# Nine unread 128x128 products placed between the products of a kernel's first chunk

## The chip, the cores and the metric

The kernel runs on one core of a Trainium2 chip. The metric is the device time of one execution in microseconds. The kernel before has a median of 508.19 us over three runs (507.17 to 508.34).

## The reference, cut to what matters

Two blocks run one after the other. The first is a delta-rule recurrence over 768 steps for 4 batches and 8 heads of 48 dimensions; the second is a feed-forward layer whose hidden value is the largest of three products.

```
k_n = k / (norm(k) + 1e-6)
for t in range(768):
    y[t]  = q[t] @ state
    v_old = state.T @ k_n[t]
    state = state + beta[t] * outer(k_n[t], v[t] - v_old)
x   = y laid out as 3072 tokens by 384
h   = max(max(x @ w1, x @ w2), x @ w3)      # 384 -> 768
out = h @ w_out                              # 768 -> 384
```

All of it is in 32-bit floating point; the weights come as 64-bit numbers, whose halves the kernel joins to 32 bits by itself.

## The kernel before, in words

The sequence is cut into 12 chunks of 64 steps. Within a chunk the recurrence becomes a triangular system: the inverse of a 64x64 triangle per head, then a few small products. Two chunks make a group of 512 tokens, and there are six groups; while the feed-forward layer of one group runs (`ffn(m)`), the recurrence of the next is threaded between its products.

The order of all instructions is written out by hand (`tc.manual_schedule()`): each engine takes its instructions in the order in which the Python code issues them. The part that matters here is the stretch before the first feed-forward group, and that group's first steps:

- `gram(n, ...)` (L404) makes the products of keys and queries (`p_g`). The last of them ahead of the stretch are those of L1343 and L1344.
- `solve(0)` (L507) eliminates in blocks of 16 on VectorE (`tmp`, L561; `y_bl`, L565), turns the result (L573), and places it in `ut` (L505).
- `halves_z(0)` and `halves_u(0)` (L676, L690) join blocks of 16 to blocks of 32 with two rounds of 64 small matmul records (`p_e`, `p_f`); `join_z(0)` and `join_u(0)` (L706, L719) join those to the inverse of 64 (`p_z`, `p_j`). Between the rounds ScalarE and VectorE copy the results out of PSUM (L688, L700, L717, L728).
- `new(0)` (L765) makes `u` (`p_u`), `to_y(0)` (L805) makes `y` (`p_y`), and `to_x(0)` (L819) turns `y` by six transposes (`p_x`) and copies it into `xt` (L839).
- `solve(1)` prepares the elimination for the second group on VectorE (L270 to L547). Its steps (L561, L565 on `y_p`) then run through the whole of the first feed-forward group.
- `ffn(0)` (L1213) starts with `hidden(0, ...)`: `p_h` (L1224) of 128x256, three matmuls (six records) for each of the three weights. The table `FIRST` (L1408) puts other work between: after the first `p_h` come `e1` (`p_e` of chunk 1) and `s0` (`p_s`, L794, with the VectorE sum into the state at L801) and two steps of `solve(1)`; after the second come `f1` (`p_f`), `k1` (`p_k`, L743, with VectorE's subtraction at L755) and three more steps.
- `weights()` (L230) joins the halves of the weights: three ScalarE operations (L247 to L249) for a piece, then one on VectorE (L259) and one on GpSimd (L263).

A 32-bit matmul stands in the profile as two records, each with its own weight load; a transpose stands as one. `ps_ffn` hands out two PSUM buffers in turn; `p_h` uses them later.

The kernel already has a helper, `busy(n, of)` (L1290), called once, with `busy(6, ident)` at L1309: six matmuls of the identity with itself into a tile `p_w` that nothing reads.

Of the kernel before, what the change touches and what calls it, by code (L numbers as in the profile page):

```python
# [23 lines left out]
def kernel(  # L24
# [31 lines left out]
    nc = tc.nc  # L56
# [10 lines left out]
    TOK = 512  # L67
# [21 lines left out]
    def ps_ffn(shape, name):  # L89
        return psum.tile(shape, FP32, name=name, tag="ffn", bufs=2)  # L90
# [10 lines left out]
    ident = const.tile([128, 128], FP32, name="ident")  # L101
# [16 lines left out]
    def rows(bb):  # L118
        return slice(C * bb, C * (bb + 1))
# [196 lines left out]
    def square(name):  # L316
        return work.tile([128, H, C], FP32, name=name, tag="square", bufs=17)
# [134 lines left out]
    def in_rows(t):  # L452
        return t.rearrange("p s r -> p (s r)")[:, 0 : BL * BL].rearrange(
            "p (j i) -> p j i", i=BL
        )
# [42 lines left out]
    def placed(cc, i, copy=nc.vector.tensor_copy, xs_of=slice(0, 2 * H)):  # L498
        bb, half = divmod(i, 2)
        r = block(bb, half)  # L500
        to = ut[cc][r, :, :, BL * half : BL * (half + 1)].rearrange(
            "p g h i -> p (g h) i"
        )
        of = in_rows(xs[0])[r, :, 16 * cc : 16 * (cc + 1)].rearrange("p i x -> p x i")
        copy(to[:, xs_of], of[:, xs_of])  # L505
# [110 lines left out]
    def both(name, w, bufs=1):  # L616
        return work.tile([128, 2, H, w], FP32, name=name, bufs=bufs)
# [6 lines left out]
    def block(bb, f=0, n=BL):  # L624
        return slice(C * bb + BL * f, C * bb + BL * f + n)

    def turn_t1(c):

        t, u_t = t1[c % NU], ut[c % NU]
        nc.vector.transpose(out=t[:, 0], in_=u_t[:, 0, :, 0:BL])  # L630
        for bb in range(2):
            nc.vector.transpose(
                out=t[block(1 - bb), 1], in_=u_t[block(bb), 1, :, 0:BL]
            )
# [4 lines left out]
    def halves_t(c, parts=(0, 1)):  # L639
        if c not in fine:  # L640
            fine[c] = [square("t") for g in range(2)]
        src = [ut[c % NU][:, g].rearrange("p h x -> p (h x)") for g in range(2)]
        dst = [t.rearrange("p h x -> p (h x)") for t in fine[c]]
        if 0 in parts:
            nc.vector.transpose(out=dst[0], in_=src[0])
        for bb in range(2) if 1 in parts else ():
            nc.vector.transpose(out=dst[1][rows(1 - bb)], in_=src[1][rows(bb)])

    def heads_of(c, name, w):


        copies = (nc.scalar.copy,) if c else (nc.scalar.copy, nc.vector.tensor_copy)
        n = H // len(copies)
        for i, copy in enumerate(copies):
            p_v = ps_two(name)[:, :, 0 : n * w]
            yield (
                range(i * n, i * n + n),
                p_v.rearrange("p g (h x) -> p g h x", x=w), copy,
            )
# [13 lines left out]
    def span(hs):  # L673
        return slice(hs[0], hs[-1] + 1)

    def halves_z(c):  # L676
        if c > 1:
            halves_t(c)
        at = [ats[2 * c + g] for g in range(2)]
        second = ut[c % NU].rearrange("p g h (f two x) -> p g h f two x", two=2, x=HB)  # L680
        for hs, p_v, copy in heads_of(c, "p_e", BL):
            for i, h in enumerate(hs):
                for bb, g in TILES:
                    r = rows(bb)
                    nc.tensor.matmul(
                        p_v[rows(bb ^ g), g, i], at[g][r, h], second[r, g, h, :, 1]
                    )
            copy(zs[c % NU][:, :, span(hs)], p_v)  # L688
# [17 lines left out]
    def join_z(c):  # L706
        at = [ats.pop(2 * c + g) for g in range(2)]
        z, second = zs[c % NU], ut[c % NU][:, :, :, BL:C]
        for hs, p_v, _ in heads_of(c, "p_z", BL):
            for i, h in enumerate(hs):  # L710
                for bb, g in TILES:
                    r = block(bb, 1)
                    nc.tensor.matmul(
                        p_v[block(bb ^ g), g, i], at[g][r, h, 0:BL], second[r, g, h]
                    )
            for bb in range(2):
                nc.scalar.copy(z[block(bb), :, span(hs)], p_v[block(bb)])  # L717
# [15 lines left out]
    def heads(t):  # L733
        return t.rearrange("p g (j two) d -> p two (g j) d", two=2)

    def times_state(kqt, i, name):
        p_b = ps_two(name)
        for j in range(NP):
            for g in range(2):
                for par in range(2):  # L740
                    for bb in range(2):
                        c0 = (g * NP + j) * D
                        nc.tensor.matmul(  # L743
                            p_b[rows(bb), par, c0 : c0 + D],
                            kqt[g][dims(par), j, bb ^ g, i],
                            st[dims(par), bb ^ g, g, j],
                        )
        return p_b[:, :, 0 : H * D].rearrange("p two (x d) -> p two x d", d=D)
# [10 lines left out]
    def old_q(c):  # L759
        kqt = [kqts[2 * c + g] for g in range(2)]  # L760
        if c:
            qs = qss[c] = both("qs", D)
            nc.scalar.copy(heads(qs), times_state(kqt, 1, "p_q"))

    def new(c):  # L765
        rhs = rhss.pop(c)
        u = us[c] = both("u", D, 2)
        for hs, p_v, copy in heads_of(c, "p_u", D):
            for i, h in enumerate(hs):
                for bb, g in TILES:  # L770
                    nc.tensor.matmul(  # L771
                        p_v[rows(bb ^ g), g, i],
                        ut[c % NU][rows(bb), g, h],
                        rhs[rows(bb), g, h],
                    )
            copy(u[:, :, span(hs)], p_v)
        if c + NU < 2 * FINE:
            for bb in range(2):
                corner = ut[c % NU][block(bb), :, :, BL:C]
                zero = kpad[0][block(bb), None, 0:1, D : D + 1]  # L780
                nc.scalar.copy(corner, zero.to_broadcast(corner.shape))
# [23 lines left out]
    def to_y(c):  # L805
        u = us[c]
        pt = [pts.pop(2 * c + g) for g in range(2)]
        y = yts[c] = both("y", D)
        for hs, p_v, copy in heads_of(c, "p_y", D):
            for i, h in enumerate(hs):  # L810
                for bb, g in TILES:
                    r = rows(bb ^ g)
                    nc.tensor.matmul(p_v[rows(bb), g, i], pt[g][r, h], u[r, g, h])  # L813
            if c:
                nc.vector.tensor_tensor(out=y, in0=qss.pop(c), in1=p_v, op=ALU.add)
            else:
                copy(y[:, :, span(hs)], p_v)

    def to_x(c):  # L819
        m, cc = divmod(c, 2)  # L820
        if m not in xts:
            xts[m] = work.tile([128, KT, TOK], FP32, name="xt")
        y_f = yts.pop(c).rearrange("p g h d -> p g (h d)")
        xt = xts[m][:, :, cc * 256 : (cc + 1) * 256].rearrange(
            "p t (g x) -> p g t x", g=2
        )
        p_x = ps_two("p_x")
        for g in range(2):
            if g and not c:
                p_x = ps_two("p_x")  # L830
            for t in range(KT):
                nc.tensor.transpose(
                    p_x[:, g, t * 128 : (t + 1) * 128],
                    y_f[:, g, t::KT],
                    ident,
                )
            of = p_x[:, :, 0 : KT * 128].rearrange("p g (t x) -> p g t x", t=KT)
            if not c:
                nc.scalar.copy(xt[:, g], of[:, g])  # L839
        if c:  # L840
            nc.scalar.copy(xt, of)
# [434 lines left out]
    def some(gen, n):  # L1276
        for _ in range(n):
            if next(gen, gen) is gen:
                break
# [7 lines left out]
    nc.vector.memset(warm, 1.0)  # L1287
    nc.scalar.sqrt(warm, warm)

    def busy(n, of):  # L1290
        p_w = ps_ffn([128, TOK], "p_w")[:, 0 : of.shape[1]]
        for _ in range(n):
            nc.tensor.matmul(p_w, ident, of)

    def keys(n, queues=one_queue, copy=nc.scalar.copy):
        gram(n, (0,), queues, copy)

# [45 lines left out]
    gram(2, (1,), None, later=True)  # L1343
    gram(3, (1,), None, later=True)  # L1344
    some(solving, HB + 1)
    halves_t(0)
    halves_z(0)
    first_norms()
# [6 lines left out]
        fetch(nc.gpsimd)  # L1355
    halves_u(0)
    turn_t1(0)
    join_z(0)
    masked(pts[0], by_par(pts[0]))
    placed(1, 2)  # L1360
# [1 line left out]
    masked(pts[1], by_par(pts[1]))  # L1362
    old_k(0)
    old_q(0)
    new(0)
    some(conv, 1)
    fetch(nc.gpsimd)
    load_v(1, nc.gpsimd)
    placed(1, 3)
    to_y(0)  # L1370
    halves_t(1)
    solving = solve(1)
    some(solving, 1)
    to_x(0)
    some(conv, 1)

# [178 lines left out]
```

## Time and profile before

| what | value |
|---|---|
| median of three runs | 508.19 us |
| the profiled execution: its own time | 506.9 us |
| the profiled execution: its span, first to last instruction | 505.2 us |
| mean granted TensorE clock over the span | 0.968 |
| TensorE matmul busy | 484.0 us (96%) |
| VectorE busy | 361.1 us (71%) |
| ScalarE busy | 169.4 us (34%) |
| GpSimd busy | 187.1 us (37%) |

The busy time of TensorE is that of its records, which overlap each other, so 96% does not say that the array is full for 96% of the time. The granted clock is the share of full speed that the clock gate lets through; the page shows it in 40 slices in tenths (9 stands for 90% or more). The chain that ended last is followed backwards from the last instruction: TensorE has 76% of it, VectorE 11%, ScalarE 4% and DMA 3%.

A row of the timeline gives the start in us, the duration of the whole row, the engine, the line, the operation with its tiles, the part of the array (rows by columns) and the size, the number of records, and, in brackets, the idle time ahead of it with the instruction that ended it.

### The profile page before, as it was taken

The numbers are of one execution on the slowest core, as the hardware profiler recorded it, in microseconds if no ns is written. First come the engines' busy times: TensorE is split into PE (matmuls) and PEld (weight loads), VectorE is DVE, ScalarE is ACT, GpSimd is POOL, SyncE is SP. The second block draws the span as 40 slices with busy tenths as digits, with TensorE's granted clock in tenths as the row PEclk, the third lists the DMA queues.
The fourth block names the chain that finished last, engine by engine and source line by source line (L and its number), as shares of the span: only waits on it lengthen the run. The fifth ranks groups of instructions, "written<-read, shape, count | busy, mean of one in ns | idle before, by whom it ended". The sixth has DMA issues, their size and how long they took to land.

```text
span 505.2 us, 18676 instructions
## 1 busy us (share of the span) xinstructions
PE 484.0 (96%) x8064; PEld 338.0 (67%) x8064; DVE 361.1 (71%) x835; ACT 169.4 (34%) x320; POOL 187.1 (37%) x311
## 2 busy tenths in 40 slices
PE   7678989999999999999999999999999999999996
PEld 6467767855566555565565565555797457998895
DVE  5888799787996441799652999565998874468753
ACT  5585664885422142210152200242201032212210
POOL 7434472793391935770395880501000020000000
PEclk9855899999999999999999999999999999999999
DMA  8937869864045934544584652744224230340002
GB/s 114 205 50 214 195 142 160 198 181 137 3 120 134 191 72 77 146 119 117 112 156 104 158 137 74 149 72 96 64 54 90 47 86 15 85 94 1 0 18 47
DMA packets 109121, 53.50 MB, mean 106 GB/s; under 512 B 92208, under 2 KB 102864, under 8 KB 109040
## 3 DMA queue, kind: packets, MB, share of 16 engines
q1 hardware_dynamic: 97280, 31.78, 31.0%
q0 software_dynamic: 9216, 19.85, 16.5%
q8 instruction: 63, 1.03, 0.9%
q10 hardware_dynamic: 2544, 0.69, 0.8%
q14 instruction: 18, 0.15, 0.1%
HBM read 39.17 MB, written 13.11 MB: 103 GB/s over the span
## 4 chain that ended last, share of the span: by engine, by line
PE 76%; DVE 11%; ACT 4%; DMA 3%; SPq 3%; issue 2%; POOL 0%; DVEq 0%; ACTq 0%; POOLq 0%
PE p_h L1224 28%; PE p_o L985 13%; PE p_o L1262 12%; PE p_c L1163 5%; DVE tmp L561 3%; PE p_g L415 2%; PE p_m L905 2%; PE p_u L771 2%; PE p_k L743 2%; DVE y_p L565 2%; DMA kmore<-in_k_dram 2%; PE p_y L813 2%; PE p_s L794 2%; PE p_q L743 1%; PE p_j L726 1%
## 5 line engine op out<-in xcount | busy, mean ns | idle before, releaser
L1224 PE MATMUL p_h<-xt,w_sb 128*128 128x512 f32 (+1 forms) x450 | 186.8, 558 | 0.6 <-ACT xt L839 0.6
L1224 PEld LDWEIGHTS p_h<-xt,w_sb 128*128 128x128 f32 x450 | 82.4, 193 | 69.2 <-issue 61.6
L1238 DVE TENSOR_TENSOR h<-h,p_h 128x512 f32<-128x512 f32 (+1 forms) x42 | 25.5, 607 | 46.8 <-PE p_h L1224 46.3
L565 DVE TENSOR_TENSOR y_bl<-y_bl,tmp 128x31 f32<-128x31 f32 (+20 forms) x139 | 50.4, 363 | 4.8
L561 DVE TENSOR_TENSOR tmp<-x_bl,y_bl 128x31 f32<-128x31 f32 (+20 forms) x139 | 48.8, 351 | 3.9
L1262 PE MATMUL p_o<-wo_sb,h 128*128 128x384 f32 x144 | 48.9, 490 | 0.0
L373 POOL DMA_DIRECT2D turned<-in_q_dram x72 | 39.3, 554 | 4.6 <-POOL turned L368 3.1
L1262 PEld LDWEIGHTS p_o<-wo_sb,h 128*128 128x128 f32 x144 | 26.7, 190 | 17.2
L1234 ACT ACTIVATE h<-p_h 128x512 f32<-128x512 f32 x24 | 14.3, 597 | 69.2 <-PE p_h L1224 69.2
L263 POOL TENSOR_TENSOR w_sb<-mant,up 128x384 int32<-128x384 int32 x18 | 19.0, 1054 | 39.5 <-DVE mant L259 37.8
L415 PEld LDWEIGHTS p_g<-kqt 48*64 48x64 f32 x1216 | 24.5, 142 | 9.2 <-issue 6.3
L415 PE MATMUL p_g<-kqt 48*64 48x64 f32 (+1 forms) x1216 | 27.7, 241 | 0.9 <-ACT kqt L344 0.8
L1268 ACT COPY o_sb<-p_o 128x384 f32<-128x384 f32 x12 | 5.8, 479 | 62.6 <-PE p_o L1262 56.5
L801 DVE TENSOR_TENSOR st<-st,p_s 48x768 f32<-48x768 f32 (+1 forms) x18 | 17.1, 949 | 12.7 <-PE p_s L794 12.4
L399 DVE TENSOR_TENSOR pt<-p_g,mask 128x512 f32<-128x512 f32 x20 | 13.8, 690 | 17.0 <-PE p_g L415 16.9
L598 POOL DMA_DIRECT2D ut<-y_d x4 | 2.6, 653 | 60.6 <-DMA y_d<-y_bl 60.6
L148 POOL DMA_DIRECT2D v_t<-in_v_dram x14 | 11.6, 832 | 35.3 <-PE p_u L771 35.3
L368 POOL MEMSET turned<- 128x96 f32 x18 | 3.3, 191 | 49.4 <-DVE kqt L389 49.4
L771 PEld LDWEIGHTS p_u<-v_t,ut 64*64 64x64 f32 x768 | 13.5, 141 | 8.4 <-issue 7.3
L432 ACT COPY at<-p_g 128x512 f32<-128x512 f32 x22 | 12.8, 585 | 17.4 <-DVE pt L399 15.4
L373 POOL DMA_DIRECT2D turned<-in_k_dram x32 | 17.5, 556 | 1.2 <-POOL turned L368 1.2
L1163 PE MATMUL p_c<-xt,w_sb 128*128 128x256 f32 x72 | 17.7, 379 | 0.0
(239 smaller groups left out, 907.3 us busy)
## 6 DMA issues: line engine op xcount, KB each, us to landing
w_bits<-in_moe_w_dram SPq DMA_DIRECT2D x9, 384.0 KB, 6.2
w_bits<-in_moe_w_dram POOLq DMA_DIRECT2D x9, 384.0 KB, 5.7
turned<-in_q_dram POOLq DMA_DIRECT2D x72, 48.0 KB, 2.8
out_dram<-o_sb SPq DMA_DIRECT2D x36, 96.0 KB, 2.3
y_x<-y SPq DMA_DIRECT2D x32, 96.0 KB, 3.0
qall<-y_x SPq DMA_DIRECT2D x32, 96.0 KB, 2.8
v_t<-in_v_dram POOLq DMA_DIRECT2D x14, 192.0 KB, 5.0
at_d<-at SPq DMA_DIRECT2D x72, 32.0 KB, 3.0
```

What stands on the lines that cost most here:

```text
L263: nc.gpsimd.tensor_tensor(out=dst.bitcast(I32), in0=mant_v.bitcast(I32), in1=up_v, op=ALU.add)
L373: (queue, nc.gpsimd)[i].dma_start(out=t[p0 : p0 + 32, bb, at : at + NP * 2 * D].rearrange("p (j x) -> p j x", j=NP), in_=(k, q)[i][2 * bb ...
L415: nc.tensor.matmul(p_g[rows(bb ^ (g * i)), par, c0 : c0 + C * (1 + whole)], kq[:, 0], kq if whole else kq[:, i],)
L561: nc.vector.tensor_tensor(out=t_v, in0=row.to_broadcast(t_v.shape), in1=column.to_broadcast(t_v.shape), op=ALU.mult,)
L565: nc.vector.tensor_tensor(out=rest, in0=rest, in1=t_v, op=ALU.subtract)
L771: nc.tensor.matmul(p_v[rows(bb ^ g), g, i], ut[c % NU][rows(bb), g, h], rhs[rows(bb), g, h],)
L801: nc.vector.tensor_tensor(out=s_v[r], in0=s_v[r], in1=p_s[r, :, 0 : H * D], op=ALU.add)
L985: nc.tensor.matmul(to[:, g], a[j][:, 128 * g : 128 * (g + 1)], b[j], start=(start and g == j == 0), stop=(stop and g == 1 and j == len(a) ...
L1163: nc.tensor.matmul(to, w[stays], moves, start=(n == 0), stop=(n == len(terms) - 1))
L1224: nc.tensor.matmul(p_h, w_sb[i][:, t, f * 128 : (f + 1) * 128], xt[:, t, lo : lo + w], start=(t == 0), stop=(t == KT - 1),)
L1238: nc.vector.tensor_tensor(out=h, in0=h, in1=p_h, op=ALU.max)
L1262: nc.tensor.matmul(p_o, stays, moves, start=(n == 0), stop=(n == len(terms) - 1))
```

## The change

The helper `busy` moves up in the function and gets the identity as its default operand. It is called five more times, with nine matmuls in all: four before `halves_t(0)`, one after `turn_t1(0)`, one before `new(0)`, one before `to_y(0)` and two before `to_x(0)`. Each is a 128x128 product of the identity with itself into a tile that nothing reads. Nothing is removed, and nothing else is moved.

```diff
+    def busy(n, of=None):
+        of = ident if of is None else of
+        p_w = ps_ffn([128, TOK], "p_w")[:, 0 : of.shape[1]]
+        for _ in range(n):
+            nc.tensor.matmul(p_w, ident, of)
...
-    def busy(n, of):
-        p_w = ps_ffn([128, TOK], "p_w")[:, 0 : of.shape[1]]
-        for _ in range(n):
-            nc.tensor.matmul(p_w, ident, of)
...
     some(solving, HB + 1)
+    busy(4)
     halves_t(0)
     halves_z(0)
...
     turn_t1(0)
+    busy(1)
     join_z(0)
...
     old_q(0)
+    busy(1)
     new(0)
...
     placed(1, 3)
+    busy(1)
     to_y(0)
...
     some(solving, 1)
+    busy(2)
     to_x(0)
```

## The prediction

> **What bounds the kernel now.** I read the page's slices first: all of the 40 slices but the first ones show the full clock.
>
> ```profile
> PE   7678989999999999999999999999999999999996
> ...
> PEclk9855899999999999999999999999999999999999
> ```
>
> The second view gives the granted clock by stretches. Every switch falls on one grid of 3.41 us (18.96, 22.37, 25.79, 53.09; 27.3 us is eight of them), so I cut the stretches there. PE, PEld, DVE, ACT and POOL have their busy us and records, then come clock, DMA share and GB/s.
>
> ```profile
> 18.96:22.37 3.41, 3.41 (x56) 2.63 (x60) 3.03 (x11) 1.52 (x3) 2.27 (x5) 0.50 1.35 224
> ...
> 25.79:29.20 3.41, 2.13 (x66) 1.80 (x64) 3.24 (x6) 3.14 (x7) 0.00 (x0) 0.50 0.47 77
> ...
> 39.44:42.85 3.41, 2.64 (x93) 2.50 (x89) 2.55 (x6) 3.31 (x7) 1.76 (x3) 0.50 0.93 332
> 42.85:46.27 3.42, 2.85 (x9) 2.27 (x10) 3.15 (x9) 2.36 (x5) 2.18 (x3) 0.50 0.71 191
> 46.27:49.68 3.41, 3.41 (x76) 2.58 (x78) 3.10 (x10) 0.41 (x2) 0.00 (x0) 0.50 0.89 197
> 49.68:53.09 3.41, 3.41 (x72) 3.05 (x65) 1.48 (x5) 2.14 (x4) 3.19 (x3) 0.50 0.84 149
> 53.09:56.51 3.42, 3.42 (x135) 2.93 (x135) 1.50 (x4) 1.54 (x5) 1.74 (x2) 1.00 0.85 234
> ```
>
> TensorE works at half speed from 25.79 to 53.09, and full speed comes back only after 49.68:53.09. The third view is TensorE's timeline there: the same `p_h` row takes 2.93 at half and 1.56 at full clock (55.71).
>
> ```profile
> 34.88 1.24 PE L713 MATMUL p_z<-ut,at 32*32 32x32 f32 x64 [0.47 <-ACT ut L700]
> 36.06 1.80 PE L726 MATMUL p_j<-z,t 32*32 32x32 f32 x64
> 38.10 2.08 PE L771 MATMUL p_u<-v_t,ut 64*64 64x48 f32 x62 [0.24 <-issue]
> ...
> 39.99 2.06 PE L813 MATMUL p_y<-u,pt 64*64 64x48 f32 x62
> 42.83 1.52 PE L832 MATMUL p_x<-ident,y 128*128 128x128 f32 x6 [0.77 <-ACT y_p L525]
> 44.92 2.93 PE L1224 MATMUL p_h<-xt,w_sb 128*128 128x256 f32 x6 [0.57 <-ACT xt L839]
> 47.77 1.93 PE L685 MATMUL p_e<-ut,at 64*64 64x32 f32 x64
> 49.50 1.94 PE L794 MATMUL p_s<-u,kpad 64*64 64x48 f32 x64
> 51.37 2.40 PE L1224 MATMUL p_h<-xt,w_sb 128*128 128x256 f32 x6
> ```
>
> Last, VectorE's timeline of 42 to 57 shows who waits for that half speed.
>
> ```profile
> 51.51 0.95 DVE L801 TENSOR_TENSOR st<-st,p_s 128x768 f32<-128x768 f32 x1 [1.89 <-PE p_s L794]
> ...
> 55.91 0.95 DVE L755 TENSOR_TENSOR v_t<-v_t,p_k 128x768 f32<-128x768 f32 x1 [1.61 <-PE p_k L743]
> ```
>
> From 42.1 to 49.6 VectorE has no idle time worth a name; then it waits 1.89 + 0.31 + 1.61 us, each time for TensorE. From 55.9 to 89.2 it is busy 31.25 of 33.30 us with `solve(1)`, and the chain runs through it; from 89.2 to 107 TensorE is busy 17.8 of 17.8 us, and 393 of 398 after. So what moves L755 should move the end by as much.
>
> **The added work.** Nine matmuls are 18 records. The `p_w` records at the start are about 0.21 us apart at half clock (the six `p_x` say (1.52 - 0.42) / 5 = 0.22), so a matmul costs 0.43 us at half and about 0.22 at full clock. `p_w` has no reader, so no other engine gets a wait; only what stands behind it in TensorE's queue can be late.
> - `busy(4)`: 8 x 0.213 = 1.7 us, from about 27.7, in the idle 2.21 us before `p_e` (30.13, waits for ACT's `ut` L505). Cost 0; without that cover 1.7.
> - `busy(1)` before `p_z`: 0.43 in 0.47 idle (waits for ACT's L700). Cost 0; uncovered 0.43.
> - Before `p_u`: 0.43 in 0.24 idle: +0.2.
> - Before `p_y`: `p_u` and `p_y` follow each other without a gap, so all of it: +0.43.
> - Before `p_x`: 0.85 in 0.77 idle, beside VectorE's copy of y (42.12, 0.56): at most +0.1.
> Sum at an unchanged clock: `p_y` ends 0.65 later, `p_x` starts 0.7 later.
>
> **What it does to the clock.** No row says what the gate counts. My estimate: the time for which the array streams in a window of the grid, 0.213 us per 128-column record at half clock, small tiles four side by side, so a quarter each. The windows of before then give: released at 0.78 (49.68:53.09: `p_s` 16 x 0.08 = 1.28 less 0.1, `p_h` 3.5 x 0.427 = 1.5) and 0.81 (18.96:22.37); not released at 0.70 (42.85:46.27 and 46.27:49.68) and less; throttled at 0.43 and 0.19; kept at 0.45 and more. The gate would open between 0.70 and 0.78 and close near 0.44. With the change:
> - 25.79:29.20 has 0.53; `busy(4)` adds 1.35 us before 29.20, so 0.93: full clock from 29.20. The first half of `p_e` takes 0.55 in place of 1.07, and ACT's z copy, the conversion behind it and L700 come 0.4 earlier (not more: `p_f` still waits for VectorE's L647 at 32.33).
> - 29.20:32.61 then holds only some 0.7 us at full clock, 0.2: half clock again from 32.61.
> - The next two stay at half: 0.48 + 0.125 each, 0.6.
> - 39.44:42.85: `p_u` 0.25, `p_w` 0.43, `p_y` 1.28, `p_w` about 0.5: 2.5 of 3.41, 0.72 to 0.75, against 0.52 before. The next: the rest of `p_w` 0.3, `p_x` 1.28, `p_h` 0.9: 0.73. Both lie in the unknown band.
> I take it that the gate opens at 42.85 or 46.27: two chances, each above all that failed.
>
> **The sum.** `p_y` ends 0.65 - 0.4 = 0.25 later, so VectorE's stream from 42.12 is 0.3 late, ready for L801 at 49.95 (49.62 + 0.3).
> Open at 42.85: `p_x` 43.1 (full: 0.95), two ACT copies of 0.48, `p_h` 44.75; then, start to start at full clock, 1.5 (`p_h`), 1.05 (`p_e`, by the 64x32 row at 53.70), 1.1 (`p_s`), 1.5 (`p_h`): 49.9. L801 runs 49.95 to 50.9, when VectorE is the last; `p_f` ends 50.95, `p_k` 52.05; VectorE needs 1.5 after L801 (four steps, L259, L1238): L755 at 52.45, 3.45 us before 55.91.
> Open at 46.27: `p_h` starts 45.2 and ends 47.3, `p_s` 49.45, L801 as above, `p_h` 50.95, `p_f` 52.0, `p_k` 53.1: L755 at 53.15, 2.75 earlier.
> Middle: -3.1. The profiled execution would take 506.9 - 3.1 = 503.8 (span 502.1). Its time is 1.3 below the median, so I take the difference over: 508.19 - 3.1 = 505.1, own range 504.4 to 506.0 (both ends, and the 1.2 us spread of the runs). What is late next is VectorE's own elimination, then TensorE.
>
> **The rivals.**
> 1. The gate opens at 49.68 (46.27:49.68 with 0.73): L755 at 54.35, 1.55 earlier, 506.6. [...]
> 2. The grid lies elsewhere in other executions. A window ending at 48.5 would hold 0.8 in the kernel before, and would open the gate there: L755 at 53.95, and only about 1.2 is left to gain: 507.0. The one profile can't tell; three runs within 1.2 us speak for a like grid. [...]
> 3. The gain is lost after 55.9: at 85.84 TensorE waits 1.01 us for a `qall` load. If that load doesn't come earlier with the rest, TensorE waits up to 3 us longer there: 507.7. Against it: SP issues that load after TensorE's `p_t` and so moves along.
> 4. No new opening, back at 53.09 as before: L755 +0.1, 508.3.
> 5. Slower: the products miss every window, 29.20 too, and their delay of 0.7 moves `p_s` and `p_h` in 49.68:53.09 so that it holds 2.5 us (`p_e` 0.25, `p_s` 1.28, `p_h` 1.0), 0.74 in place of 0.78. If the gate needs more than that, it opens at 56.51: `p_h` ends 54.4, `p_f` 56.25, `p_k` 57.45, L755 at 57.5, +1.6: 509.8. For it: the band is not known within 0.70 to 0.78.
>
> **How the numbers follow.** Forecast (505.1) 0.52; rival 1 0.12; 2 0.08; 3 0.08; 4 0.10; 5 0.10. A difference of 0.3%, 1.5 us, is about what a measurement can tell here. Faster by more: 0.52 and half of rival 1, 0.58. Slower by more: 0.10. Within: 0.32. The range leaves out rival 5 and a little at the low end (a clock held from 29.20 on would give some 503): 503.8 to 508.9.
>
> **What would show it.** Granted clock 1.00 in 29.20:32.61 and from 42.85 or 46.27; `p_w` rows in the gaps; `p_y` some 0.25 later; L801 near 50 without a wait for `p_s`; L755 near 52.8; `solve(1)`'s last copy (L569, 88.53) 3 us earlier, and the end too. Wrong if the clock comes back at 53.09 or later, or if L569 is early and TensorE idles between 85 and 107.

## The result and the profile after

The changed kernel is slower: a median of 510.80 us over 22 runs against 507.45 us for the kernel before in 22 runs beside it, a ratio of 1.0074 with a 95% interval of 1.0055 to 1.0093. The forecast was 505.1 us. Its profiled execution took 509.84 us (span 508.1), 2.94 us more than that of before.

The page of the changed kernel (the clock's slices, the queue that carries instructions, the chain of waits, and the group of `p_u`):

```profile
PEclk9755989999999999999999999999999999999999
...
q8 instruction: 63, 1.03, 0.9%
...
PE 90%; DMA 3%; DVE 1%; issue 1%; SPq 1%; ACT 1%; POOL 0%; POOLq 0%; DVEq 0%; ACTq 0%
...
L778 PE MATMUL p_u<-v_t,ut 64*64 64x48 f32 x768 | 15.2, 227 | 3.4 <-issue 3.4
```

The half clock is not shorter in all. Its long stretch now runs from 26.20 to 50.10 (25.79 to 53.09 in before), but the one ahead of it is longer (15.96 to 22.79, against 18.96 to 22.38), and a third has come (67.16 to 70.58): 34.1 us together, against 30.7. The chain now lies on TensorE for 90% and not for 76%. The last line matters most: `p_u` has 3.4 us of idle time ahead of it that ends with nothing but its own "issue". In before the same group had 1.2 us of it.

TensorE's timeline of the changed kernel around the added products (start, duration of the row, then the row; in brackets the idle time ahead). Line numbers from L673 on are 7 higher than in before:

```profile
27.26 2.07 PE L681 MATMUL p_w<-ident 128*128 128x128 f32 x8
...
38.42 1.96 PE L778 MATMUL p_u<-v_t,ut 64*64 64x48 f32 x64
40.31 0.79 PE L681 MATMUL p_w<-ident 128*128 128x128 f32 x2
41.03 1.96 PE L820 MATMUL p_y<-u,pt 64*64 64x48 f32 x64
42.92 1.22 PE L681 MATMUL p_w<-ident 128*128 128x128 f32 x4
43.94 1.49 PE L839 MATMUL p_x<-ident,y 128*128 128x128 f32 x6
45.99 2.93 PE L1231 MATMUL p_h<-xt,w_sb 128*128 128x256 f32 x6 [0.57 <-ACT xt L846]
...
55.35 0.45 PE L750 MATMUL p_k<-st,kqt 48*64 48x48 f32 x15 [0.57 <-issue]
...
66.22 0.78 PE L778 MATMUL p_u<-v_t,ut 64*64 64x48 f32 x35 [1.64 <-issue]
```

Two things are to be seen. A single added product sets the next row back by 0.72 us (40.31 to 41.03), not by 0.43. And two rows of small products are split in two by a stop that no other engine causes. In before the second of them was split too, by a shorter stop:

```profile
63.73 0.91 PE L771 MATMUL p_u<-v_t,ut 64*64 64x48 f32 x47
65.65 0.49 PE L771 MATMUL p_u<-v_t,ut 64*64 64x48 f32 x17 [1.01 <-issue]
```

The changed kernel's granted clock by stretches, on its own grid, which lies 0.4 us later than that of before:

```profile
26.20:29.62 3.42, 3.13 (x40) 2.72 (x40) 3.32 (x4) 3.37 (x7) 0.00 (x0) 0.50 0.56 90
...
46.68:50.10 3.42, 3.42 (x54) 2.48 (x55) 3.07 (x12) 1.08 (x3) 0.00 (x0) 0.50 0.59 133
50.10:53.51 3.41, 3.41 (x140) 2.92 (x136) 2.31 (x8) 2.17 (x4) 2.79 (x3) 1.00 0.85 155
63.75:67.16 3.41, 1.77 (x68) 1.43 (x67) 3.31 (x8) 1.85 (x5) 0.92 (x2) 1.00 0.41 122
67.16:70.58 3.42, 3.42 (x18) 2.39 (x20) 2.97 (x8) 3.35 (x7) 3.06 (x5) 0.50 0.34 55
```

Full clock comes at 50.10, one window earlier than before's 53.09, and 29.62 opened nothing. The window 63.75:67.16, in which the stop of 1.64 us lies, is busy for 1.77 us only, and the next window is at half clock again.

The landmarks of the two profiled executions, in us:

| event | before | after |
|---|---|---|
| first `p_e` | 30.13 | 29.64 |
| first `p_h` | 44.92 | 45.99 |
| VectorE's subtraction from `v_t` (L755, after L762) | 55.91 | 55.91 |
| last copy of the first group's elimination (L569) | 88.53 | 89.72 |
| last `p_h` of the first group | 99.50 | 99.75 |
| first `p_o` after the row at 114 | 140.12 | 142.17 |
| end of the span | 505.20 | 508.13 |

Up to 99.75 only 0.25 us is lost. 1.80 us is lost before 142.17, and 0.88 behind it (there, another stop of 0.34 us ends at 180.76). Most of the 1.80 us seems to lie in one place; TensorE's timeline there, in after and then in before:

```profile
113.34 1.13 PE L778 MATMUL p_u<-v_t,ut 64*64 64x48 f32 x58
116.24 0.33 PE L778 MATMUL p_u<-v_t,ut 64*64 64x48 f32 x6 [1.77 <-issue]
```
```profile
113.10 1.20 PE L771 MATMUL p_u<-v_t,ut 64*64 64x48 f32 x64
114.24 2.84 PE L1224 MATMUL p_h<-xt,w_sb 128*128 128x512 f32 x6
```

The chain of waits of the changed kernel counts the stop in full (start, us, what):

```profile
113.42 1.06 PE p_u L778 x58
114.47 1.77 issue
116.24 0.33 PE p_u L778 x4
```

It also reaches the other engines. ScalarE's copy of `u` starts at 116.61 in place of 114.71, and behind it VectorE begins the chain of the next elimination (first row after, second row before):

```profile
117.60 0.18 DVE L271 TENSOR_SCALAR nt_bl<-root_bl 128x32 f32<-128x32 f32 x1 [4.14 <-ACT root_bl L270]
```
```profile
115.70 0.18 DVE L271 TENSOR_SCALAR nt_bl<-root_bl 128x32 f32<-128x32 f32 x1 [2.48 <-ACT root_bl L270]
```

**What the stop is.** I numbered TensorE's instructions in every trace: matmuls, weight loads and the sequencer's semaphore instructions together, in order of start. The stops fall behind the same numbers in every kernel: 193 + 256 k. I call such a place an edge. In before, the stop in `p_u` at 65.65 is behind number 2753, 47 records into the row; in after, it is behind number 2753 again, but 29 records into the row, because 18 added records (36 instructions) went ahead. The stop at 114.47 is behind 4801. The queue that the page calls "instruction" moves 1.03 MB in 63 packets of 16,384 bytes; TensorE has 16,297 instructions in after, and 63 x 256 is 16,128. The two kernels below with 256 more TensorE instructions have exactly one packet more; the page of the second of them:

```profile
q8 instruction: 64, 1.05, 0.9%
```

From these counts I take it that TensorE's program comes by DMA in blocks of 256 instructions, one packet each, and that the stop is the wait for the next block. In all 16 profiles there are 41 stops at these numbers in which the next instruction starts 0.55 us or more after the last one ahead of the edge, with TensorE idle between the two. Every one has "issue" for its reason, and every one ends 1.26 to 1.89 us after the end of the block's packet. Some of them:

| kernel | behind instruction | reached | packet | goes on | after the packet's end |
|---|---|---|---|---|---|
| before | 2753 | 64.42 | 62.88 to 64.38 | 65.65 | 1.27 |
| after | 2753 | 64.36 | 63.60 to 64.91 | 66.22 | 1.31 |
| after | 4801 | 114.25 | 113.83 to 114.76 | 116.24 | 1.48 |
| late9 | 4801 | 113.65 | 112.70 to 113.62 | 114.99 | 1.37 |
| shift18 | 1985 | 49.36 | 48.48 to 49.97 | 51.86 | 1.89 |
| nine_shift128 | 961 | 24.42 | 25.29 to 27.00 | 28.58 | 1.57 |

In before, number 4545 is passed at 112.53 and 4801 at 117.08, 4.55 us later, with a `p_h` row of 2.84 us between: no stop. In after, the 36 instructions put the same two numbers at 110.42 and 114.25, with 122 of the 128 records between in `p_j` and `p_u`: 3.83 us, and the block is not there: its packet ends at 114.76, 0.51 us behind the edge.

### The profile page after: what moved, and what is told of

Read it like the earlier page. It is cut to its first block, busy times and chain, and to the rows that moved or that the text cites. A ratio compares the mean times of both kernels' runs of the same rounds, so it can differ in the third digit from the quotient of the medians.

```text
span 508.1 us, 18712 instructions
## 1 busy us (share of the span) xinstructions
PE 490.6 (97%) x8082; PEld 343.1 (68%) x8082; DVE 361.2 (71%) x835; ACT 169.1 (33%) x320; POOL 186.7 (37%) x311
## 3 DMA queue, kind: packets, MB, share of 16 engines
q8 instruction: 63, 1.03, 0.9%
## 4 chain that ended last, share of the span: by engine, by line
PE 90%; DMA 3%; DVE 1%; issue 1%; SPq 1%; ACT 1%; POOL 0%; POOLq 0%; DVEq 0%; ACTq 0%
PE p_h L1231 35%; PE p_o L992 13%; PE p_o L1269 12%; PE p_c L1170 5%; PE p_g L415 4%; PE p_u L778 3%; PE p_y L820 3%; PE p_m L912 2%; PE p_k L750 2%; PE p_q L750 2%; PE p_s L801 2%; DMA kmore<-in_k_dram 2%; PE p_j L733 2%; PE p_z L720 1%; DMA qall<-in_q_dram 1%
## 5 line engine op out<-in xcount | busy, mean ns | idle before, releaser
L1241 ACT ACTIVATE h<-p_h 128x512 f32<-128x512 f32 x24 | 14.3, 597 | 69.7 <-PE p_h L1231 69.7
L778 PE MATMUL p_u<-v_t,ut 64*64 64x48 f32 x768 | 15.2, 227 | 3.4 <-issue 3.4
```

The source lines that it names most:

```text
L778: nc.tensor.matmul(p_v[rows(bb ^ g), g, i], ut[c % NU][rows(bb), g, h], rhs[rows(bb), g, h],)
```

## The experiments

My theory after the result: the records as such cost the time, since they move the block edges along the program. The rivals: the products' array time and delay ahead of the first `p_h`; or the clock. All kernels ran in five rounds. None leaves out any of the reference's computation. Every ratio is to the kernel before, in the same rounds.

**shift18 and shift128.** The kernel before, with small products early, ahead of the `p_t` transposes at about 23 us: nine (18 records) or 64 (128 records, one whole block).

```diff
+    def small_products(n):
+        p_w = ps_ffn([128, TOK], "p_w")
+        for i in range(n):
+            r = block(*divmod(i % 4, 2))
+            nc.tensor.matmul(p_w[r, 0:BL], ident[r, r], ident[r, r])
...
+    small_products(9)     # 64 in shift128
     turn(3, (1,))
```

> The kernel before with nine small unread products (32x32x32, 18 records, 36 instructions of TensorE) in an idle gap at 23 us, and none of the nine of the change. Theory A (TensorE's instructions come in blocks of 256; the change moves every block's edge by 36 instructions, and two edges fall into runs of small matmuls): as slow as the changed kernel, 510 to 511.5 us against 507.5, with p_u stopping after 29 records at 64.6 and after 58 records at 114. Theory B (the unread products change what the clock gate does): 507.5, since they take hardly any array time. Theory C (the products stand in the way of p_u, p_y and p_x): 507.5.

> The kernel before with 64 small unread products at 23 us: 128 records, 256 instructions, one whole block. Theory A: the edges lie again where they lay, so 507.0 to 508.0, p_u stopping after 47 records as before. Theories B and C: 507.5. What it tells: if it is slow, the small products cost time where they stand, and the other runs with them can't be read as shifts.

shift18: 510.31 us against 508.44, ratio 1.0038 (1.0010 to 1.0066). Slower with none of the change's products, and the stop is in the same `p_u` row, at 115.09 behind its 58th record, 1.22 us. Its gate opened at 43.6, yet L755 came only 0.94 us earlier after `p_e` than in before (24.84 against 25.78). TensorE's timeline of shift18 shows a likely reason:

```profile
51.86 0.33 PE L794 MATMUL p_s<-u,kpad 64*64 64x48 f32 x8 [2.28 <-issue]
...
56.23 0.45 PE L743 MATMUL p_k<-st,kqt 48*64 48x48 f32 x15 [0.73 <-issue]
```

At full clock the rows of small products run faster (the `p_e` row at 47.62 takes 1.14 us, the one at 47.77 in before 1.93) and come to their edges sooner, and two stops, 2.28 and 0.73, lie where the gain would be.

shift128: 510.65 against 508.44, 1.0045 (1.0018 to 1.0072). I expected no change: a miss. Its profile (507.25 us, the fastest of its 12 runs) has no stop at 114, as the theory wants, but stops of 0.42 at 961, inside the added row, and of 1.5 behind 2753. What makes the other runs slower can't be read from it. So the place of the edges alone doesn't give the time of a kernel.

**nine_shift128 and nine_small.** The changed kernel with 55 small products at the same place (73 products in all, so that later edges stand as in before, a block on); and the changed kernel with each of its nine products cut to 32x32x32.

```diff
+    small_products(55)
     turn(3, (1,))
```
```diff
-    busy(4)
+    small_products(4)     # and the other four calls likewise
```

> The changed kernel with 55 more small unread products at 23 us, so that all additions together are 128 records, one whole block. Theory A: the 1.8 us stop at 114 is gone, and the time falls to 505 to 508. Theory B: what the nine do to the clock stays: 510 to 511.5. Theory C: their place on the path stays: 510 to 511.5.

> The changed kernel with each of its nine 128x128 products cut to 32x32x32, in the same five places: the same 18 records, hardly any array time. Theory A: still slow, 510 to 511.5. Theory B and theory C: back to 507.5 (within 1).

nine_shift128: 511.48 against 508.44, 1.0062 (1.0032 to 1.0093). I expected 505 to 508: a miss. It has no stop at 114, as the theory wants, but it can't be used as a test, for its added row stops for 3.97 us by itself, and three more stops of 1.00 to 1.54 us follow up to 69.56:

```profile
23.61 1.00 PE L1301 MATMUL p_w<-ident 32*32 32x32 f32 x95
28.58 0.32 PE L1301 MATMUL p_w<-ident 32*32 32x32 f32 x15 [3.97 <-issue]
```

nine_small: 510.99 against 508.44, 1.0055 (1.0030 to 1.0079). With the records kept and nearly all of the array time gone (the first call's eight records take 0.33 us, 2.07 in after), nearly all of the loss stays. From `p_e` to the first `p_h` it still takes 16.31 us (14.79 in before, 16.35 in after). This speaks against the array time. Its one profile doesn't show the edge at 114 as the cause, though: the stop there is 0.29 us, and `p_e` starts 2.22 us later than in before.

**late9, late2, only4, last5.** The kernel before with nine or two small products at about 95 us, where TensorE waits for nothing and the clock is full; then the changed kernel with only its first call, and with only the other four calls.

```diff
         if i == 16:
+            small_products(9)     # 2 in late2
```
```diff
     busy(4)      # kept in only4, gone in last5
...
-    busy(1)      # the three of them, and busy(2): gone in only4, kept in last5
```

> The kernel before with nine small unread products (18 records, 36 instructions) at about 95 us, behind a p_h and ahead of a p_g in the first feed-forward group; nothing of the change. All that comes earlier is as before. Theory A (the edges of TensorE's blocks of 256 instructions move): p_u near 114 stops after 58 of its 64 records for 1.2 to 1.8 us, and the kernel is 1.2 to 2.2 us slower than before, 0.25 to 0.45%. If edges play no part: at most 0.3 us slower.

> The same with two small products (4 records) at the same place. Theory A: the edge that lies 12 records behind that p_u moves to 8 records behind it, still behind the long p_h, so no stop, and the time is that of before within 0.2%. If it is as slow as with nine, the cause is a product at that place, and not the edge.

> The changed kernel with the first four products alone, in TensorE's idle time before p_e; the five others are taken out. Theory A: 8 records, the edge comes to lie within the p_h behind that p_u, a stop of at most 0.5 us, so 0 to +0.5 us. Theory C (the other five stand in the way): no cost, 0. Theory B (the products change the clock for the better): 0 to -1 us.

> The changed kernel without its first four products; the five between p_f, p_z, p_j, p_u, p_y and p_x stay. Theory C: the first p_h of the feed-forward layer starts 1.1 to 1.5 us later after p_e than before (16.0 to 16.3 us in place of 14.8). Theory A adds a stop of 0.5 to 1.3 us near 114, since the edge lies two records behind that p_u. Together 1.5 to 2.8 us slower than before, less what an earlier opening of the gate gives back (up to 0.8).

| kernel | this, us | before, us | ratio, interval | stop in `p_u` at 114 | first `p_o` to the end, us |
|---|---|---|---|---|---|
| late9 | 509.76 | 508.01 | 1.0038 (1.0011 to 1.0065) | 1.13 | 366.64 |
| late2 | 508.24 | 508.01 | 1.0009 (0.9988 to 1.0029) | none | 365.15 |
| only4 | 509.01 | 508.01 | 1.0011 (0.9992 to 1.0030) | none | 366.56 |
| last5 | 510.85 | 508.01 | 1.0053 (1.0032 to 1.0074) | none; 0.39 in `p_h` behind it | 366.56 |

late9 has nothing of the change near the first chunk, and shows the stop of the changed kernel; late2, at the same place, doesn't. TensorE's timeline of late9, then of late2:

```profile
112.74 1.13 PE L771 MATMUL p_u<-v_t,ut 64*64 64x48 f32 x59
114.99 0.32 PE L771 MATMUL p_u<-v_t,ut 64*64 64x48 f32 x5 [1.13 <-issue]
```
```profile
112.74 1.21 PE L771 MATMUL p_u<-v_t,ut 64*64 64x48 f32 x64
113.88 2.84 PE L1224 MATMUL p_h<-xt,w_sb 128*128 128x512 f32 x6
```

The row starts at the same 112.74, so the stop is made by the nine's 18 records, not by their time. The last column is not explained by this stop: only4 takes 366.56 without it, and the one edge stop of note in that stretch is 0.41 us, at 262.68; in late9 it is 1.22 us, at 180.40. The intervals of late9 and late2 overlap, so the times alone would not tell the two apart. only4 shows the one part of the clock step that came as forecast, the opening by the first call:

```profile
25.98:29.40 3.42, 3.42 (x72) 3.26 (x64) 3.29 (x5) 3.40 (x7) 0.00 (x0) 0.50 0.35 58
29.40:32.81 3.41, 2.57 (x108) 2.04 (x110) 3.20 (x8) 2.62 (x6) 0.00 (x0) 1.00 0.42 67
32.81:36.22 3.41, 2.86 (x130) 2.44 (x124) 2.94 (x8) 2.97 (x11) 3.00 (x3) 0.50 0.08 12
```

One window at full clock, then half again until 53.3. last5 carries most of the loss: its `p_e` to first `p_h` takes 16.15, and its stops are 1.34 behind 2241, 0.61 behind 2753, 0.39 at 116.85 (0.5 to 1.3 expected) and 0.79 at 184.9.

**nine_wide, last5_wide, first4_wide, start_wide.** The same products, drawn together into matmuls with a wider moving operand, so that the array does the same work in fewer records. The six at the start are drawn together too, which gives records back: nine_wide has 2 more than before (not 18), last5_wide the same number as before. first4_wide has the first call alone, as one wide matmul, with the start as it was (2 more). start_wide is the kernel before with only its start drawn together (8 fewer).

```diff
+    def wide(n):
+        p_w = ps_ffn([128, TOK], "p_w")[:, 0 : 128 * n]
+        nc.tensor.matmul(
+            p_w.rearrange("p (n x) -> p n x", x=128), ident,
+            ident[:, None, :].to_broadcast([128, n, 128]),
+        )
...
-    busy(6, ident)
+    wide(4)
+    wide(2)
...
-    busy(4)
+    wide(4)      # and the other four calls likewise
```

> The changed kernel with the same 128x128 products in the same places, but several of one place drawn into one matmul of 512 or 256 columns, and the six at the start too: two records more than before in place of 18. Theory A (edges) and C (path) together: the stop at 114 and the later ones go, what the five cost on the path stays: 0.25 to 0.45% slower than before, half of the change's loss. A alone: no slower than before. C alone (edges play no part): 0.6 to 0.8% slower.

> The five products between p_f and p_x alone, in wide form, and the start in wide form: exactly as many records as before, so every edge stays. Theory C: the first p_h starts 16.0 to 16.4 us after p_e in place of 14.8, and the kernel is 0.2 to 0.4% slower. A alone: as fast as before.

> The first four products alone as one wide matmul ahead of p_e: two records more than before, no edge to speak of moved, nothing in the way. Theory B's gain, if there is one, stands here by itself: -0.1 to 0%. A and C: no difference.

> The control: the kernel before with only the six products at the start in wide form, eight records fewer. Theory A: the edges move by eight records the other way; the one near 114 goes further away from p_u, into the p_g behind it. No difference (within 0.15%).

| kernel | this, us | before, us | ratio, interval | gate open from | `p_e` to first `p_h`, us |
|---|---|---|---|---|---|
| nine_wide | 508.34 | 507.44 | 1.0012 (0.9994 to 1.0029) | 50.9 | 16.21 |
| last5_wide | 507.57 | 507.44 | 1.0007 (0.9985 to 1.0029) | 43.3 | 15.22 |
| first4_wide | 507.48 | 507.44 | 0.9997 (0.9978 to 1.0016) | 54.0 | 14.80 |
| start_wide | 507.24 | 507.44 | 0.9986 (0.9969 to 1.0004) | 43.1 | 14.26 |

The same array work without the records: most of the loss is gone (1.0012 against 1.0074; last5_wide 1.0007 against last5's 1.0053; I expected 1.0025 to 1.0045 and 1.002 to 1.004), and so is the stop at 114. The delay ahead of the first `p_h` is still there in nine_wide (16.21), so that delay is not the main part of what makes the changed kernel slow. A reservation: the start is also changed in two of the three wide kernels with products, and start_wide alone gives 0.9986, not distinct from 1. Against start_wide, which has the same start and ran in the same rounds, nine_wide's median is 0.22% higher and last5_wide's 0.07%. So some of the 0.74%, perhaps a third, can still be the products' array work and delay. No wide kernel with products is free of stops; nine_wide has its largest behind 2753, where before has 1.01:

```profile
63.51 0.90 PE L785 MATMUL p_u<-v_t,ut 64*64 64x48 f32 x45
67.10 0.55 PE L785 MATMUL p_u<-v_t,ut 64*64 64x48 f32 x19 [2.69 <-issue]
```

start_wide's one profile suggests what an early gate is worth when no stop stands in its way: open from 43.1, L755 23.36 us after `p_e` (25.78 in before), and the end at 503.66. TensorE's timeline of start_wide, without a stop from `p_h` to `p_k`:

```profile
45.42 1.56 PE L1231 MATMUL p_h<-xt,w_sb 128*128 128x256 f32 x6 [0.61 <-ACT xt L846]
...
51.61 1.15 PE L750 MATMUL p_k<-st,kqt 48*64 48x48 f32 x64
```

**nine_same and start_one.** An attempt to hold the number of records exactly: the start as one wide matmul of four, with the nine products wide (0 more than before), and without them (10 fewer).

```diff
-    busy(6, ident)
+    wide(4)
```

> The changed kernel's nine products in wide form, and at the start four products in one matmul in place of six: exactly as many records as before, every edge from the first feed-forward group on where it lay (the run with two records more had a new stop of 0.7 us at instruction 5057, in a p_g near 123). If the shift of the edges is the whole loss: within 0.15% of before, and from the first p_o to the end 365.0 to 365.2 us as before. If the five on the path cost what they delay the first p_h (1.4 us): 0.2 to 0.35% slower. If the products open the gate earlier for a gain: faster, up to -0.3%.

> The kernel before with four products in one matmul at the start in place of six: ten records fewer, nothing of the change. The edge at instruction 2753, which stops p_u near 65 us for 0.5 to 1.3 us in nearly every profile, moves to ten records later, and the one near 114 to 22 records behind its p_u. Theory A: 0 to 0.25% faster than before. If edges play no part: no difference.

nine_same: 508.94 against 508.74, 1.0031 (0.9999 to 1.0063). start_one: 509.57 against 508.74, 1.0026 (0.9995 to 1.0057). Both are inconclusive. Between the two, nine_same's nine wide products cost nothing that can be seen (508.94 against 509.57). In both profiles the gate first opened at 14.3 us and not near 5.5, and `p_e` started 1.7 to 2.3 us later than in before. Whether the four products at the start, in place of six, are to blame can't be told: nine_small, whose start is unchanged, first opened at 14.7. I expected start_one to be faster, and it isn't; its profile has stops of 2.11 behind 705 and 1.27 at 120.06, behind 4801. nine_same's has 2.93 behind 705, 1.67 behind 2241 and 1.49 behind 2753.

## Why the prediction was wrong

**Two steps failed.** The middle of the forecast had the subtraction at L755 at 52.8 and the end 3.1 us earlier. L755 came at 55.91, as in before, and the end 2.93 us later. So 3.1 us of the miss lie ahead of L755, in the step "What it does to the clock" and in costs on the path that were priced too low; the other 2.93 us lie behind it, in "The added work".

**The added work: a term was left out.** It priced the nine products by their array time and by who waits behind them, and so had nothing to price after 55.9 us. It left out that 18 records are 36 instructions, and that every later block edge then falls at another place of the program. The runs make a table of two causes:

| kernel | array work of the nine | records added | ratio |
|---|---|---|---|
| after | yes | 18 | 1.0074 |
| nine_small | nearly none | 18 | 1.0055 |
| shift18, late9 | none | 18 | 1.0038 each |
| nine_wide | yes | 2 | 1.0012 |
| nine_same | yes | 0 | 1.0031, inconclusive |
| late2 | none | 4 | 1.0009 |
| shift128 | none | 128 | 1.0045 |

By the times, most of the loss goes with the records: the intervals of after (from 1.0055) and nine_small (from 1.0030) lie above that of nine_wide (to 1.0029). By the profiles, the edge makes the stop at 114: late9 has it and late2 has not. How much of the 2.93 us that one stop costs is less certain. From the start of that `p_u` row to the first `p_o`, before takes 27.0 us and after 28.8, which gives the 1.80; but the profiles with no stop at an edge in that stretch take 26.8 to 28.2. That the edges make the rest of the loss is argued and not shown, and shift128 speaks against the edges as the only cause. The row that should have been asked stood in before: 1.01 us of "issue" idle time within a row of 64 alike `p_u` records, at 65.65. I passed over it, since nothing was released there.

**What bounds the kernel: right where no stop follows.** In start_wide L755 came 1.39 us earlier than in before (54.52), and the end 1.54 earlier (503.66). But in nine_wide L755 came 0.23 earlier and the end 2.17 later: a stop of 2.69 us follows at 67.10.

**The cost on the path: too small.** `busy(4)` was hidden, as said: `p_e` still waits 0.3 us for ScalarE behind it. But `p_z` came 0.38 later after `p_e`, not 0; `p_u` 0.8, not 0.2; `p_x` and the first `p_h` 1.6, not 0.7. The pair of 128x128 records ahead of `p_y` held up that row by 0.72 us at half clock (40.31 to 41.03 in after, 41.54 to 42.26 in last5), while I took 0.43 from records that follow their like. This error is not the main loss: nine_wide keeps the delay and has 1.0012 (0.22% against start_wide).

**The clock: the estimate failed.** The opening at 29.20 came in only4 (29.40), but not in after, where by the prediction's estimate the window 26.20:29.62 held 0.75 (1.70 us of `p_w`, 0.85 of `p_g`). It didn't come in first4_wide either, where 26.66:30.07 held 0.85 (1.07 of `p_w`, 1.71 of `p_g`, 0.13 of `p_t`). In start_wide 39.69:43.10 held 0.63 (0.87 of `p_u`, 1.28 of `p_y`) and opened the gate. So the estimate doesn't sort the windows that open the gate from those that don't, and the band of 0.70 to 0.78, on which the forecast rested, is not borne out. What the gate counts stays open. The second opening came at 50.10, later than either forecast (42.85, 46.27). It is the opening of rival 1 (49.68, on a grid 0.41 us later), but L755 came at 55.91 and not at 54.35. Whether the six transposes of `p_x` are counted, as the estimate had them (1.28 us), this profile can't tell: 43.27:46.68 held 0.72 with them, and opened nothing. Rival 2 was largely right. The grid was not at the same place in the three profiles compared (the first switch at 5.31 in before, 5.7 in after, 4.9 in late9), and the gate opened early and late both in kernels with the products (43.3 in last5_wide, 54.0 in first4_wide) and without (43.1 in start_wide, 52.7 in late9). Whether the products open the gate earlier on average stays open: one profile of each kernel can't tell.

**The sum: the gain was there in part, and was taken back.** From the first `p_h` to L755 the changed kernel needs 9.92 us, not 10.99. Of that 1.07 us gain, and 0.49 of an earlier `p_e`, the 1.56 us of delay ahead of the first `p_h` leave nothing: L755 at 55.91 in both. The size of the forecast gain was plausible: 2.4 us in start_wide's profile for an opening at 43.1, where 3.45 had been worked out for 42.85.

**Rivals 3, 4 and 5.** TensorE's wait for `qall` loads went from 3.6 to 3.2 us in all, and the 1.01 us at 85.84 are gone, so rival 3 played no part. Rival 4 (no new opening) wasn't the case. The time came out beyond rival 5's 509.8, but not by its mechanism: the gate did not open late.

**What stays open.** Why shift128 is slow, though its profile shows the later edges where before has them. And why a packet starts 0.65 us after the edge before it in one case (before, behind 4545) and 3.4 us in another (after, the same number): the `w_out` loads were on the DMA queues in that stretch of both kernels (four issues of 384 KB between 109 and 116 us in before, five in after). And what the gate counts.

## What to carry to other kernels

Count the instructions that a change adds to TensorE's stream, and not only their time: here 18 added records moved the edge at 2753 from behind the 47th record of its `p_u` row to behind the 29th, and put the one at 4801 into the row at 114, where TensorE stood for 1.77 us. Idle time that ended with "issue" in the middle of a row of like records was the sign of such an edge (1.01 us in before, 1.64 and 1.77 in after); number the engine's instructions, and see whether the stops lie 256 or a multiple of it apart, as they did here (2753 and 4801 are 2048 apart). Where filler products are wanted, try drawing them into one wide matmul, so that the number of records stays near what it was (nine_wide 1.0012 with 2 more, after 1.0074 with 18 more).

## What the runs showed of the hardware that I had not expected

- TensorE's stops lay behind instructions 193 + 256 k, and the queue "instruction" moved 63 packets of 16,384 bytes, 64 with 256 more instructions. TensorE went on 1.26 to 1.89 us after the end of the block's packet (41 stops in 16 profiles). The longest stop was 3.97 us (nine_shift128), in a row of 110 records of 32x32.
- A row of 64 small records (128 instructions) took 0.75 us (`p_j` at 112.42 in before) to 1.20 us (`p_u` at 113.10) at full clock. By my estimate from these two rows, two such rows behind each other use up a block in 1.5 to 2.4 us; 3.83 us were too short at 114 in after. The `p_h` row of 2.84 us at 114.24 in before is only 12 instructions, and the edge at its end (4801, passed at 117.08) cost nothing.
- Two windows with little work were followed by half clock, one emptied by a stop and one not: in after 63.75:67.16 was busy for 1.77 us, with 1.64 us lost to a stop, and in start_wide 56.75:60.17 for 1.91 us, with no stop at an edge; in both the next 3.41 us were at half clock.
